# First 512 tokens by wide transposes: K-pair matmul groups over four banks and a chain of weight loads on the ACT queue, in a TensorE-bound kernel

## Chip, cores, metric

One core of one Trainium2 chip. The metric is the device time of one execution in microseconds, as a median over runs. The profile's own span of the same execution is about 1.7 to 2.2 us shorter (487.74 against 486.0 us for the kernel before), so spans are compared only with spans and device times only with device times.

## The reference, cut to what matters

```python
x = A_x                                        # 2048 tokens x 1024, bf16
g = sigmoid((x * gate_w).sum(-1))
a = linear_attention(x, A_wqkv) @ A_wo         # 32 heads of 32
b = dilated_local_attention(x, B_wqkv) @ B_wo  # window 8, dilation 2
out = g * a + (1 - g) * b
```

The kernel begins with the v projection of block B: `x @ B_wqkv[:, 2048:3072]`. It contracts over 1024 channels, in eight steps of 128 (called d here), so x has to stand transposed in SBUF, channels on the partitions. One matmul takes 128 tokens of one d as its stationary operand and 512 output columns as its moving one. 16 token tiles x 2 column halves x 8 steps make 256 matmuls for this projection.

## The kernel before

All operations are declared with a cost, an estimated transfer time and a priority. A list scheduler in Python, run when the kernel is built, orders each engine's queue by these numbers. So a change of costs or of priorities can reorder any engine. Transfers (DMA) are issued by the engines SP and ACT, each in its own queue. TensorE (PE) writes its sums to PSUM, which is used here in banks of 128 x 512 sums.

```python
def load_x(t, prio):          # one tile of 128 tokens, all eight d
    return P.op("sp", lambda e: e.dma_start_transpose(xT[:, :, t*128:(t+1)*128], x2[...]), 1.5, ..., lat=1.3)

load_x(0, 0)
load_w(0, 0, Bw, 2048, 0.1, 0, 2, "act")       # first weight half in pairs of d:
load_w(0, 0, Bw, 2048, 0.2, 2, 4, "act")       # two on the ACT queue,
load_w(0, 0, Bw, 2048, 0.3, 4, 6)              # two on the SP queue
load_w(0, 0, Bw, 2048, 0.4, 6, 8)
for t in range(1, NT):
    load_x(t, 3 + t)
for d in range(0, 8, 2):
    load_w(0, 1, Bw, 2560, 6.1 + 0.1*d, d, d + 2)   # second weight half, SP queue, behind x tile 3
...
for i in range(WARM):                          # WARM = 11 dummy matmuls
    P.op("pe", lambda e: e.matmul(banks[7].ap(), warm[:, 0:128], warm[:, :], start=True, stop=True), ...)
...
for t, half in [(4*b + i, half) for b in range(NT//4) for half in range(2) for i in range(4)]:
    bank = main.next()
    step = 2 if t == 0 else 8
    for d in range(0, 8, step):
        o = group(bank, xs, w, [...], d, d + step)
    ...
# much later: 16 small copies into zsel, and four "folds" woven into the next projection
            if n in (2, 4, 6, 8):
                fold((n - 2) // 4, (n - 2) // 2 % 2)
```

Four tiles go through the first column half, then the same four through the second, and so on. A tile of x is 256 KB, and so is a pair of d of a weight half. A pair of d is called a K-pair below, when the matmuls on it are meant. The late part belongs to block A: "kv" matmuls (az with pk), then the four folds of 16 small matmuls each (w with kvT), then "den" matmuls that read the tile zsel.

Of the kernel before, what the change touches and what calls it, by code (L numbers as in the profile page):

```python
# [13 lines left out]
D = 1024  # L14
# [1102 lines left out]
def build_kernel(nc, A_x, A_wqkv, A_wo, B_x, B_wqkv, B_wo, gate_w, out):  # L1117
    del B_x
    S = A_x.shape[1]
    NT = S // 128  # L1120
    HS = S // 2
    x2 = A_x[0].rearrange("(m e) d -> e m d", e=2)
# [5 lines left out]
    def SB(shape, dtype, name, at=None):  # L1128
        n = SZ[dtype]
        for d in shape[1:]:  # L1130
            n *= d
        if at is None:
            at = base[0]
            base[0] += (n + 31) // 32 * 32
        uid[0] += 1
        h = nc.alloc_sbuf_tensor_at("%s_%d" % (name, uid[0]), list(shape), dtype, offset=at)
        return Tile("S", h, at, list(shape), dtype)
# [38 lines left out]
    xT = SB([128, 8, S], BF16, "xT")  # L1176
    qT = SB([128, 8, S], BF16, "qT")
    kT = SB([128, 8, S], BF16, "kT")
    ws = [SB([128, 8, 1024], BF16, "w%d" % i) for i in range(4)]
# [12 lines left out]
    zsel = SB([128, 8, 32], BF16, "zsel")  # L1192
    kva = SB([128, 8, 33], F32, "kva")
# [25 lines left out]
    gwb = SB([128, 1024], BF16, "gwb", at=pk.t[3].lo)  # L1219
    xn = Ring([SB([128, 1024], BF16, "xn%d" % i, at=az.t[i].lo) for i in range(2)])  # L1220
# [7 lines left out]

    FILL = 0.2
    PVLAG = 3  # L1230
    WARM = 11
    PASSES = 6
    mm = lambda n: max(n / 2400.0, 0.0267) + 0.0025
    act = lambda n: 0.19 + n / 1200.0
    dps = lambda n: 0.14 + n / 960.0

    def plan(seen):

        P = Prog(nc, nc.alloc_semaphore)
# [63 lines left out]
        Bw = B_wqkv.rearrange("(dc p) f -> p dc f", p=128)  # L1303
        Bo = B_wo.rearrange("(dc p) f -> p dc f", p=128)

        def load_x(t, prio):
            e_, r = t // 8, t % 8
            return P.op("sp", lambda e: e.dma_start_transpose(xT[:, :, t * 128:(t + 1) * 128], x2[e_, r * 128:(r + 1) * 128, :]),  # L1308
                        1.5, writes=[xT.part((0, 8), (t * 128, (t + 1) * 128))], prio=prio, chan="x%d" % t, lat=1.3)

        def load_w(slot, half, src, c0, prio, d0=0, d1=8, eng="sp", after=()):
            n = d1 - d0
            return P.op(eng, lambda e: e.dma_start(ws[slot][:, d0:d1, half * 512:half * 512 + 512], src[:, d0:d1, c0:c0 + 512]), 0.4 + 0.2 * n,  # L1313
                        writes=[ws[slot].part((d0, d1), (half * 512, half * 512 + 512))], prio=prio, chan="w%d_%d_%d" % (slot, half, d0), lat=0.55 * n, after=after)

        load_x(0, 0)
        load_w(0, 0, Bw, 2048, 0.1, 0, 2, "act")
        load_w(0, 0, Bw, 2048, 0.2, 2, 4, "act")
        load_w(0, 0, Bw, 2048, 0.3, 4, 6)
        load_w(0, 0, Bw, 2048, 0.4, 6, 8)  # L1320
        for t in range(1, NT):
            load_x(t, 3 + t)
        for d in range(0, 8, 2):
            load_w(0, 1, Bw, 2560, 6.1 + 0.1 * d, d, d + 2)
        P.op("sp", lambda e: e.dma_start(gwb[:, :], gate_w[None, :].to_broadcast([128, D])), 0.6, writes=[gwb.all()], prio=29, chan="gw", lat=0.8)


        main = Pool(banks[0:7])

        def group(bank, lhs, rhs, reads, lo=0, hi=8):  # L1330
            def fn(e):
                last = None
                for dc in range(lo, hi):
                    last = e.matmul(bank.ap(), lhs(dc), rhs(dc), start=(dc == 0), stop=(dc == 7))  # L1334
                return last
            return P.op("pe", fn, (hi - lo) * mm(512), reads=reads, writes=[bank.iv])
# [13 lines left out]
        def x_tile(t):  # L1350
            return (lambda dc: xT[:, dc, t * 128:(t + 1) * 128]), xT.part((0, 8), (t * 128, (t + 1) * 128))
# [4 lines left out]
        def w_half(slot, half):  # L1356
            return (lambda dc: ws[slot][:, dc, half * 512:half * 512 + 512]), ws[slot].part((0, 8), (half * 512, half * 512 + 512))
# [13 lines left out]

        for i in range(WARM):
            P.op("pe", lambda e: e.matmul(banks[7].ap(), warm[:, 0:128], warm[:, :], start=True, stop=True), 0.43, reads=[warm.all()], writes=[banks[7].iv], prio=-1)


        early = {(2, 0): (1, 0, Bw, 1024, 21), (4, 1): (2, 0, Bw, 0, 22), (7, 1): (1, 1, Bw, 1536, 23), (10, 1): (2, 1, Bw, 512, 24),
                 (12, 1): (3, 0, Aw, 1024, 25), (14, 1): (3, 1, Aw, 1536, 26)}
        for t, half in [(4 * b + i, half) for b in range(NT // 4) for half in range(2) for i in range(4)]:
            vt, vs = vst.next()
            xs, xr = x_tile(t)  # L1380
            bank = main.next()
            w, wr = w_half(0, half)
            step = 2 if t == 0 else 8
            for d in range(0, 8, step):
                o = group(bank, xs, w, [xr, ws[0].part((d, d + step), (half * 512, half * 512 + 512))], d, d + step)
            move(vt[:, :, 0:32], lambda bank=bank: bank.ap().rearrange("p (h d) -> p h d", d=32), 512, bank, vt.part((0, 16), (0, 32)))
            P.op("sp", lambda e, t=t, vt=vt, half=half: e.dma_start(vB_hbm[t * 128:(t + 1) * 128, half * 528:half * 528 + 528], vt[:, :, :].rearrange("p h d -> p (h d)")), 0.6, reads=[vt.all()],
                 writes=[hb(t * 128, (t + 1) * 128, half)], chan="vst%d" % vs, lat=0.5, prio=5)
            if (t, half) in early:
                load_w(*early[t, half], after=[o])  # L1390
        load_w(0, 0, Aw, 2048, 30)
        load_w(0, 1, Aw, 2560, 31)


        for t in range(NT):
            xt, xs_ = xn.next()
            P.op("sp", lambda e, t=t, xt=xt: e.dma_start(xt[:, :], x2[t // 8, (t % 8) * 128:(t % 8) * 128 + 128, :]), 0.6, writes=[xt.all()], chan="xn%d" % xs_, lat=1.0)
            P.op("dve", lambda e, t=t, xt=xt: e.scalar_tensor_tensor(out=xt[:, :], in0=xt[:, :], scalar=1.0, in1=gwb[:, :], op0=ALU.mult, op1=ALU.mult,
                                                                      accum_out=gt[:, t:t + 1]), dps(1024), reads=[xt.all(), gwb.all()], writes=[xt.all(), gt.part((t, t + 1))],
                 prio=1000 + len(P.ops) + 80)  # L1400
# [7 lines left out]
        main = Pool(banks[0:4])  # L1408
# [109 lines left out]
        for e_ in range(2):  # L1518
            if True:
                for j in range(8):  # L1520
                    for isq in range(2):
                        for u in (2 * e_, 2 * e_ + 1):
                            bank = main.next()
                            w, wr = w_cols(1 + isq, j)
                            xs, xr = x_chunk(u)
# [10 lines left out]
        for c in range(4):  # L1536
            for I in range(2):
                P.op("sp", lambda e, c=c, I=I: e.dma_start(ws[1][32 * c:32 * c + 32, 4 * I:4 * I + 4, :],
                                                           A_wo[512 * I + 128 * c:512 * I + 128 * c + 128, :].rearrange("(r e) f -> e r f", e=32)), 0.6,
                     writes=[ws[1].part((4 * I, 4 * I + 4), (0, 1024))], prio=40, chan="wo%d_%d" % (c, I), lat=0.9)  # L1540
# [27 lines left out]
        for t in range(NT):  # L1568
            pkt, _ = pk.next()
            azt, _ = az.next()  # L1570
            xs, xr = x_tile(t)
            for r in range(4):
                bank = main.next()
                w, wr = w_half((3, 0)[r // 2], r % 2)
# [16 lines left out]
        main = Pool(banks)  # L1591
# [5 lines left out]
        for c in range(4):  # L1597
            for r in range(4):
                k = 4 * (c % 2) + r
                P.op("dve", lambda e, c=c, r=r, k=k: e.tensor_copy(zsel[32 * r:32 * r + 32, c:8:4, k:k + 1], kva[32 * c:32 * c + 32, r:8:4, 32:33]), 0.1,  # L1600
                     reads=[kva.all()], writes=[zsel.all()])

        def fold(I, jh):
            four = [main.next() for _ in range(4)]

            def fn(e):
                for r in range(4):
                    for c in range(4):
                        sl = 4 * I + r
                        last = e.matmul(four[c].ap()[32 * r:32 * r + 32, :], kvT[32 * c:32 * c + 32, 32 * sl:32 * sl + 32],  # L1610
                                        ws[1][32 * c:32 * c + 32, sl, jh * 512:(jh + 1) * 512], start=True, stop=True, tile_position=(32 * c, 32 * r))
                return last
            P.op("pe", fn, 0.3, mode="t", reads=[kvT.all(), ws[1].part((4 * I, 4 * I + 4), (jh * 512, jh * 512 + 512))], writes=[b.iv for b in four], name="fold")
            for c in range(4):
                move(ws[1][:, 4 * I + c, jh * 512:(jh + 1) * 512], four[c].ap, 512, four[c], ws[1].part((4 * I + c, 4 * I + c + 1), (jh * 512, jh * 512 + 512)))
# [92 lines left out]
        for n, (u, j) in enumerate(nums):  # L1708
            numer(u, j)
            if j == 7 and u % 2:  # L1710
                after(3, lambda u=u: over(u - 1, u))
            slot(0)
            if n in (2, 4, 6, 8):
                fold((n - 2) // 4, (n - 2) // 2 % 2)
            if n >= 20:
                a_out(*outs.pop(0))
                slot(0)
# [44 lines left out]
    P, flag_op = best[:2]  # L1762
# [55 lines left out]
```

## Time and profile before

| | before |
|---|---|
| device time, median | 487.27 us (487.18 to 487.52, 6 runs) |
| span of the profiled run | 486.0 us |
| TensorE (PE) busy | 474.7 us, 98% |
| first useful matmul | 6.25 us |
| last matmul ends | 483.0 us |

Two lines of the profile page: the busy time of each engine with its share of the span, and the shares by engine of the chain of work that ended last.

```profile
PE 474.7 (98%) x4339; PEld 223.0 (46%) x4403; DVE 285.2 (59%) x547; ACT 140.2 (29%) x227; POOL 5.9 (1%) x36
...
PE 95%; DVE 2%; issue 1%; DMA 1%; SPq 0%; ACT 0%
```

TensorE is busy nearly all the time and holds 95% of the chain. The change can only win back its idle time, or time in which it works without use.

The timeline of TensorE in the first 22 us (start, length, line, operation, shapes, number merged; in brackets the idle time before it and what ended it):

```profile
1.25 4.61 PE L1373 MATMUL ps_all<-warm 128*128 128x512 bf16 x11 [1.25 <-DVE warm L1283]
6.25 2.02 PE L1334 MATMUL ps_all<-w,xT 128*128 128x512 bf16 x8 [0.39 <-DMA xT<-in_A_x_dram]
8.51 6.65 PE L1334 MATMUL ps_all<-w,xT 128*128 128x512 bf16 x30 [0.24 <-DMA xT<-in_A_x_dram]
15.38 6.85 PE L1334 MATMUL ps_all<-w,xT 128*128 128x512 bf16 x31 [0.23 <-DMA w<-in_B_wqkv_dram]
```

The first line is the dummies: 11 matmuls start 0.43 us apart. Useful matmuls start 0.216 us apart once the clock is at full rate. These two spacings are how the clock shows in the timeline: 0.43 us is half rate. The next lines begin after short waits: for the first x, for the next x, for the weights' second half. (The trace lacks one matmul record in fifty: it has 251 of this projection's 256.)

The same view around the folds:

```profile
317.73 0.43 PE L1610 MATMUL ps_all<-w,kvT 32*32 32x512 bf16 x16
318.09 3.63 PE L1334 MATMUL ps_all<-xT,w 128*128 128x512 bf16 x16
322.22 0.44 PE L1610 MATMUL ps_all<-w,kvT 32*32 32x512 bf16 x16 [0.50 <-DVE pq L1347]
```

PE sat idle for 0.50 us before the second fold, and what ended it was a VectorE operation on the tile pq.

### The profile page before, as it was taken

To read this page: it belongs to the slowest core of one execution; us is meant where nothing else is said; L and a number is where in the kernel's file an instruction comes from. 1 tells how busy PE (TensorE), PEld (TensorE's weight loads), DVE (VectorE), ACT (ScalarE), POOL (GpSimd) and SP (SyncE) were. 2 spreads that over 40 slices of the span, in tenths; PEclk is the share of its full clock that TensorE was granted. 3 is DMA by queue.
4 is the path that set the end of the run, shared out by engine and by line. 5 is a ranking of instruction groups with operands and counts; after the bars stand their busy time and mean duration, and the time that the engine had idled before them with its cause. 6 is when DMAs were issued, how large, how long until landed. Compare 5 with 4: busy or idle time off the path is not lost.

```text
span 486.0 us, 10106 instructions
## 1 busy us (share of the span) xinstructions
PE 474.7 (98%) x4339; PEld 223.0 (46%) x4403; DVE 285.2 (59%) x547; ACT 140.2 (29%) x227; POOL 5.9 (1%) x36
## 2 busy tenths in 40 slices
PE   8999999999999999999999999999999999999997
PEld 3444444444444444454544454434444444444443
DVE  2121435888688888575666566496578236653434
ACT  2111121235322234334433333454532230111000
POOL 4000000000000000000000000000000000000000
PEclk9999999999999999999999999999999999999999
DMA  8999992232014459333222322810085018840212
GB/s 217 225 198 308 352 365 59 66 109 86 1 44 138 107 133 255 86 81 87 57 69 69 82 66 69 213 41 2 10 228 152 1 15 237 224 23 3 88 67 89
DMA packets 72951, 57.39 MB, mean 118 GB/s; under 512 B 37953, under 2 KB 60865, under 8 KB 72898
## 3 DMA queue, kind: packets, MB, share of 16 engines
q1 hardware_dynamic: 72210, 56.07, 43.7%
q8 instruction: 36, 0.59, 0.5%
q10 hardware_dynamic: 688, 0.59, 0.4%
q14 instruction: 17, 0.14, 0.1%
HBM read 34.49 MB, written 13.76 MB: 99 GB/s over the span
## 4 chain that ended last, share of the span: by engine, by line
PE 95%; DVE 2%; issue 1%; DMA 1%; SPq 0%; ACT 0%
PE ps_all L1334 78%; PE ps_all L1693 11%; PE ps_all L1463 2%; PE ps_all L1440 2%; DMA xT<-in_A_x_dram 1%; PE ps_all L1556 1%; DVE zsel L1600 1%; PE ps_all L1638 0%; DVE pq L1347 0%; SPq L1308 0%; DVE w L1365 0%; PE ps_all L1610 0%; SPq L1313 0%; ACT e L1341 0%; DVE e L1345 0%
## 5 line engine op out<-in xcount | busy, mean ns | idle before, releaser
L1334 PE MATMUL ps_all<-w,xT 128*128 128x512 bf16 x925 | 208.6, 379 | 4.1 <-issue 2.1
L1334 PE MATMUL ps_all<-xT,w 128*128 128x512 bf16 x746 | 166.3, 379 | 2.1 <-issue 1.4
L1334 PEld LDWEIGHTS ps_all<-w,xT 128*128 128x128 bf16 x960 | 91.4, 98 | 110.6 <-DMA xT<-in_A_x_dram 1.8
L1334 PEld LDWEIGHTS ps_all<-xT,w 128*128 128x128 bf16 x768 | 73.7, 98 | 88.9 <-issue 1.3
L1693 PE MATMUL ps_all<-w,qT 128*128 128x512 bf16 (+1 forms) x259 | 55.3, 372 | 0.3
L1693 PEld LDWEIGHTS ps_all<-w,qT 128*128 128x128 bf16 x264 | 25.9, 98 | 29.6
L1365 DVE CAST vst<-ps_all 128x512 bf16<-128x512 f32 x15 | 10.4, 694 | 43.6 <-PE ps_all L1334 43.6
L1345 DVE TENSOR_SCALAR e<-e 128x512 bf16<-128x512 bf16 x64 | 18.4, 290 | 27.7 <-ACT e L1343 15.1
L1448 ACT ACTIVATE E<-ps_all 128x1824 bf16<-128x1824 f32 (+1 forms) x18 | 30.4, 1688 | 13.4 <-PE ps_all L1440 11.7
L1697 DVE SCALAR_TENSOR_TENSOR o<-ps_all,gm,xT 128x512 bf16<-128x512 f32 (+1 forms) x25 | 18.0, 728 | 21.2 <-PE ps_all L1693 21.1
L1341 ACT ACTIVATE e<-ps_all 128x512 bf16<-128x512 f32 x32 | 19.1, 597 | 39.0 <-PE ps_all L1334 38.3
L1343 ACT ACTIVATE e<-ps_all 128x512 bf16<-128x512 f32 x32 | 19.1, 597 | 32.4 <-PE ps_all L1334 32.4
L1295 DVE TENSOR_TENSOR mx<-mx,kT 128x1024 bf16<-128x1024 bf16 x32 | 20.9, 688 | 10.4 <-ACT kT L1366 10.4
L1295 DVE TENSOR_TENSOR mx<-mx,qT 128x1024 bf16<-128x1024 bf16 x32 | 20.8, 688 | 8.0 <-ACT qT L1369 8.0
L1451 DVE TENSOR_TENSOR E<-E,msk 128x1824 bf16<-128x1824 bf16 (+1 forms) x18 | 19.9, 1104 | 7.8 <-ACT E L1448 7.4
L1366 ACT ACTIVATE vst<-ps_all 128x512 bf16<-128x512 f32 x17 | 10.2, 600 | 48.0 <-PE ps_all L1334 48.0
L1480 DVE TENSOR_TENSOR ot<-ps_all,rs 128x512 bf16<-128x512 f32 x36 | 23.3, 686 | 0.0
L1366 ACT ACTIVATE az<-ps_all 128x512 bf16<-128x512 f32 x22 | 13.2, 600 | 34.5 <-PE ps_all L1334 34.5
L1366 ACT ACTIVATE kT<-ps_all 128x512 bf16<-128x512 f32 x20 | 11.9, 596 | 38.2 <-PE ps_all L1334 38.2
L1347 DVE SCALAR_TENSOR_TENSOR pk<-ps_all,e 128x512 bf16<-128x512 f32 x32 | 21.9, 689 | 0.7
L1369 ACT ACTIVATE qT<-ps_all 128x512 bf16<-128x512 f32 x19 | 11.3, 597 | 37.4 <-PE ps_all L1334 37.3
L1369 ACT ACTIVATE xT<-ps_all,g 128x512 bf16<-128x512 f32 x10 | 6.9, 687 | 45.1 <-PE ps_all L1334 45.1
(72 smaller groups left out, 261.1 us busy)
## 6 DMA issues: line engine op xcount, KB each, us to landing
rb<-rc_hbm SPq DMA_DIRECT2D x32, 256.0 KB, 5.0
w<-in_A_wqkv_dram SPq DMA_DIRECT2D x6, 1024.0 KB, 8.6
v<-vB_hbm SPq DMA_DIRECT2D x36, 132.0 KB, 2.8
vB_hbm<-vst SPq DMA_DIRECT2D x32, 132.0 KB, 6.0
w<-in_B_wqkv_dram SPq DMA_DIRECT2D x4, 1024.0 KB, 8.8
xn<-in_A_x_dram SPq DMA_DIRECT2D x16, 256.0 KB, 2.8
out_dram<-o SPq DMA_DIRECT2D x15, 256.0 KB
oB_hbm<-ot SPq DMA_DIRECT2D x36, 96.0 KB, 2.3
```

Source lines behind the costliest of these rows:

```text
L1295: P.op("dve", lambda e, m=m, op=op: e.tensor_tensor(m[:, 0:n], m[:, 0:n], src, op), 0.08 + n / 1920.0, reads=[m.all(), reg], writes=[m.all()],
L1334: last = e.matmul(bank.ap(), lhs(dc), rhs(dc), start=(dc == 0), stop=(dc == 7))
L1341: P.op("act", lambda e: e.activation(e_[:, :], bank.ap(), ACT.Exp), act(512), reads=[bank.iv], writes=[e_.all()])
L1343: P.op("act", lambda e: e.activation(e_[:, :], bank.ap(), ACT.Exp, accum_out=qe[:, col:col + 1]), act(512) + 0.1, reads=[bank.iv], writes= ...
L1345: P.op("dve", lambda e: e.tensor_scalar(e_[:, :], e_[:, :], 1.0, 1e-6, op0=ALU.min, op1=ALU.add), 0.25, reads=[e_.all()], writes=[e_.all()])
L1347: P.op("dve", lambda e: e.scalar_tensor_tensor(out=dst, in0=bank.ap(), scalar=0.0, in1=e_[:, :], op0=ALU.max, op1=ALU.add), dps(512), read ...
L1366: fa = lambda e: e.activation(dst, src(), ACT.Copy)
L1369: fa = lambda e: e.activation(dst, src(), ACT.Copy, scale=scale)
L1448: P.op("act", lambda e: e.activation(E[:, 0:32 * nq].rearrange("p (j q) -> p j q", j=4), ps[:, 4:8, 0:8 * nq], ACT.Exp), act(32 * nq), rea ...
L1451: P.op("dve", lambda e: e.tensor_tensor(ev(), ev(), m[:, :, :].rearrange("p r q -> p (r q)")[:, None, :].to_broadcast([128, 16, 2 * nq]), ...
L1480: P.op("dve", lambda e, r=r, bv=bv, h=h: e.tensor_tensor(o[:, 512 * h:512 * h + 512].rearrange("p (k i c) -> p k i c", k=2, c=32), bv()[:, ...
L1693: last = e.matmul(bank.ap(0, f1 - f0), qT[:, dc, t * 128:(t + 1) * 128], ws[3][:, dc, f0:f1], start=(dc == 0), stop=(dc == 7))
```

## The change

The intent: start useful work as soon as an eighth of the data is there. The first 512 tokens come by four wide transposes, each of 512 tokens x two steps of d. PE takes them pair of d by pair of d, for four token tiles in four PSUM banks. The weight pairs are issued on the ACT queue, the third when the first has landed, the fourth when the second has landed, and the second half right behind the fourth. Eight tiles, not four, go through the first half before the second is needed. There are 8 dummies in place of 11. At the other end, the zsel copies get a lower priority and the folds come one step later.

```diff
-    WARM = 11
+    WARM = 8
...
-        load_x(0, 0)
-        load_w(0, 0, Bw, 2048, 0.1, 0, 2, "act")
...
+        o_w = []
         for d in range(0, 8, 2):
-            load_w(0, 1, Bw, 2560, 6.1 + 0.1 * d, d, d + 2)
+            o_w.append(load_w(0, 0, Bw, 2048, 0.1 + 0.1 * d, d, d + 2, "act", o_w[-2:-1]))
+            P.op("sp", lambda e, d=d: e.dma_start_transpose(xT[:, d:d + 2, 0:512], x2[0, 0:512, 128 * d:128 * d + 256]),
+                 1.3, writes=[xT.part((d, d + 2), (0, 512))], prio=d / 2, chan="xd%d" % d, lat=1.2)
+        for t in range(4, 8):
+            load_x(t, 4 + t)
...
-        for t, half in [(4 * b + i, half) for b in range(NT // 4) for half in range(2) for i in range(4)]:
+        for t, half in [(t, half) for t0, n in ((0, 8), (8, 4), (12, 4)) for half in range(2) for t in range(t0, t0 + n)]:
...
+            if t < 4 and half == 0:
+                if t == 0:
+                    first = [main.next() for _ in range(4)]
+                    for d in range(0, 8, 2):
+                        for t_ in range(4):
+                            o = group(first[t_], x_tile(t_)[0], w, [...], d, d + 2)
+                    for d in range(0, 8, 4):
+                        load_w(0, 1, Bw, 2560, 3 + 0.1 * d, d, d + 4, "act", o_w[-1:])
+                bank = first[t]
+            else: ...
+                if (t, half) == (5, 0):          # x tiles 8 to 15, gate loads: only after this group
+                    x_op = o
+                    for t_ in range(8, NT):
+                        load_x(t_, 4 + t_, [o])
...
-                P.op("dve", ... zsel copy ..., 0.1, ...)
+                P.op("dve", ... zsel copy ..., 0.16, ..., prio=1000 + len(P.ops) + 100)
...
-            if n in (2, 4, 6, 8):
-                fold((n - 2) // 4, (n - 2) // 2 % 2)
+            if n in (3, 5, 7, 9):
+                fold((n - 3) // 4, (n - 3) // 2 % 2)
```

(Also changed: the estimated transfer times that the list scheduler uses, and the place of one later weight load.)

More of the change, by code (lines that the diff above doesn't have):

```diff
@@ L1304, in plan, with load_x @@
         Bo = B_wo.rearrange("(dc p) f -> p dc f", p=128)
-        def load_x(t, prio):
+        def load_x(t, prio, after=()):
             e_, r = t // 8, t % 8
             return P.op("sp", lambda e: e.dma_start_transpose(xT[:, :, t * 128:(t + 1) * 128], x2[e_, r * 128:(r + 1) * 128, :]),
-                        1.5, writes=[xT.part((0, 8), (t * 128, (t + 1) * 128))], prio=prio, chan="x%d" % t, lat=1.3)
+                        1.5, writes=[xT.part((0, 8), (t * 128, (t + 1) * 128))], prio=prio, chan="x%d" % t, lat=1.15, after=after)
         def load_w(slot, half, src, c0, prio, d0=0, d1=8, eng="sp", after=()):
@@ L1313, in load_w @@
             return P.op(eng, lambda e: e.dma_start(ws[slot][:, d0:d1, half * 512:half * 512 + 512], src[:, d0:d1, c0:c0 + 512]), 0.4 + 0.2 * n,
-                        writes=[ws[slot].part((d0, d1), (half * 512, half * 512 + 512))], prio=prio, chan="w%d_%d_%d" % (slot, half, d0), lat=0.55 * n, after=after)
-        load_x(0, 0)
-        load_w(0, 0, Bw, 2048, 0.1, 0, 2, "act")
-        load_w(0, 0, Bw, 2048, 0.2, 2, 4, "act")
-        load_w(0, 0, Bw, 2048, 0.3, 4, 6)
-        load_w(0, 0, Bw, 2048, 0.4, 6, 8)
-        for t in range(1, NT):
-            load_x(t, 3 + t)
-        for d in range(0, 8, 2):
-            load_w(0, 1, Bw, 2560, 6.1 + 0.1 * d, d, d + 2)
-        P.op("sp", lambda e: e.dma_start(gwb[:, :], gate_w[None, :].to_broadcast([128, D])), 0.6, writes=[gwb.all()], prio=29, chan="gw", lat=0.8)
+                        writes=[ws[slot].part((d0, d1), (half * 512, half * 512 + 512))], prio=prio, chan="w%d_%d_%d" % (slot, half, d0), lat=0.42 * n, after=after)
+        o_w = []
+        for d in range(0, 8, 2):
+            o_w.append(load_w(0, 0, Bw, 2048, 0.1 + 0.1 * d, d, d + 2, "act", o_w[-2:-1]))
[3 more added lines that the diff above has]
+            load_x(t, 4 + t)
         main = Pool(banks[0:7])
@@ L1373, in plan @@
             P.op("pe", lambda e: e.matmul(banks[7].ap(), warm[:, 0:128], warm[:, :], start=True, stop=True), 0.43, reads=[warm.all()], writes=[banks[7].iv], prio=-1)
-        early = {(2, 0): (1, 0, Bw, 1024, 21), (4, 1): (2, 0, Bw, 0, 22), (7, 1): (1, 1, Bw, 1536, 23), (10, 1): (2, 1, Bw, 512, 24),
+        early = {(1, 1): (1, 0, Bw, 1024, 21), (4, 1): (2, 0, Bw, 0, 22), (7, 1): (1, 1, Bw, 1536, 23), (10, 1): (2, 1, Bw, 512, 24),
                  (12, 1): (3, 0, Aw, 1024, 25), (14, 1): (3, 1, Aw, 1536, 26)}
-        for t, half in [(4 * b + i, half) for b in range(NT // 4) for half in range(2) for i in range(4)]:
+        for t, half in [(t, half) for t0, n in ((0, 8), (8, 4), (12, 4)) for half in range(2) for t in range(t0, t0 + n)]:
             vt, vs = vst.next()
             xs, xr = x_tile(t)
-            bank = main.next()
             w, wr = w_half(0, half)
-            step = 2 if t == 0 else 8
-            for d in range(0, 8, step):
-                o = group(bank, xs, w, [xr, ws[0].part((d, d + step), (half * 512, half * 512 + 512))], d, d + step)
+            if t < 4 and half == 0:
[3 more added lines that the diff above has]
+                        for t_ in range(4):
+                            o = group(first[t_], x_tile(t_)[0], w, [xT.part((d, d + 2), (t_ * 128, t_ * 128 + 128)), ws[0].part((d, d + 2), (0, 512))], d, d + 2)
+                    for d in range(0, 8, 4):
+                        load_w(0, 1, Bw, 2560, 3 + 0.1 * d, d, d + 4, "act", o_w[-1:])
+                bank = first[t]
+            else:
+                bank = main.next()
+                o = group(bank, xs, w, [xr, ws[0].part((0, 8), (half * 512, half * 512 + 512))])
+                if (t, half) == (5, 0):
+                    x_op = o
+                    for t_ in range(8, NT):
+                        load_x(t_, 4 + t_, [o])
             move(vt[:, :, 0:32], lambda bank=bank: bank.ap().rearrange("p (h d) -> p h d", d=32), 512, bank, vt.part((0, 16), (0, 32)))
@@ L1390, in plan @@
                 load_w(*early[t, half], after=[o])
+        P.op("sp", lambda e: e.dma_start(gwb[:, :], gate_w[None, :].to_broadcast([128, D])), 0.6, writes=[gwb.all()], prio=29, chan="gw", lat=0.8, after=[x_op])
         load_w(0, 0, Aw, 2048, 30)
@@ L1396, in plan @@
             xt, xs_ = xn.next()
-            P.op("sp", lambda e, t=t, xt=xt: e.dma_start(xt[:, :], x2[t // 8, (t % 8) * 128:(t % 8) * 128 + 128, :]), 0.6, writes=[xt.all()], chan="xn%d" % xs_, lat=1.0)
+            P.op("sp", lambda e, t=t, xt=xt: e.dma_start(xt[:, :], x2[t // 8, (t % 8) * 128:(t % 8) * 128 + 128, :]), 0.6, writes=[xt.all()], chan="xn%d" % xs_, lat=1.0, after=[x_op])
             P.op("dve", lambda e, t=t, xt=xt: e.scalar_tensor_tensor(out=xt[:, :], in0=xt[:, :], scalar=1.0, in1=gwb[:, :], op0=ALU.mult, op1=ALU.mult,
@@ L1599, in plan @@
                 k = 4 * (c % 2) + r
-                P.op("dve", lambda e, c=c, r=r, k=k: e.tensor_copy(zsel[32 * r:32 * r + 32, c:8:4, k:k + 1], kva[32 * c:32 * c + 32, r:8:4, 32:33]), 0.1,
-                     reads=[kva.all()], writes=[zsel.all()])
+                P.op("dve", lambda e, c=c, r=r, k=k: e.tensor_copy(zsel[32 * r:32 * r + 32, c:8:4, k:k + 1], kva[32 * c:32 * c + 32, r:8:4, 32:33]), 0.16,
+                     reads=[kva.all()], writes=[zsel.all()], prio=1000 + len(P.ops) + 100)
         def fold(I, jh):
```

## The prediction

> **What bounds the kernel now.** TensorE. The engine table has it busy 474.7 of 486.0 us (98%), the chain of waits is 95% PE. In the timeline, 512-column matmuls start 0.216 us apart from 15.38 us to the end at 483.0 us. A change of the first loads can only win back idle PE time, about 11 us: the head; some forty gaps of 0.16 us around the attention blocks; one of 0.50 us at 322 us; 3 us of tail. The change touches the head and the piece at 322 us.
>
> **The head before, from the timeline and the DMA issues.** Eleven dummy matmuls run from 1.25 to 5.86 us, 0.43 us apart, at half rate; the rate doubles at about 5.5 us. The first transpose of x (issued at 0.80 us) lands at 6.20 us, the weight pairs at 3.65, 6.01, 6.77 and 7.62 us, the next transposes at 8.47, 9.49 and 10.51 us. Useful work starts at 6.25 us. The 38 matmuls to 15.38 us take 9.13 us; at 0.216 us they need 8.2. So three waits (a weight pair at 7.6, x at 8.5, the weights' second half at 15.1 us) cost 0.9 us.
>
> **What the change does.**
> - A wide transpose is 256 KB in the same 256-byte packets (1,024 for an old one), so I expect the old issue cost, 1.25 to 1.4 us, and about 1 us of transfer.
> - After the first pair of x and weights there are 32 matmuls over four banks, 8 per pair: 1.73 us of PE for 512 KB. Transposes can be issued every 1.3 us and DMA moved 250 to 300 GB/s there, so pairs land every 1.3 to 1.8 us, about as fast as PE eats them. The third and fourth weight pair wait for the first and second (3.65 and 6.0 us), early enough.
> - The second weight half is first needed 64 matmuls (13.8 us) after the start, not 32: the wait at 15.1 us goes.
> - The first weight pairs and transpose are issued at the same times as before; only the third weight pair no longer contends. I expect the first landing at 5.3 to 6.2 us, estimate 5.8: a gain of 0.4 us.
> - Eight dummies end at about 4.7 us. The Trainium skill ("TensorE: Matmul & The Clock Gate", Part 1) says that activity in a free-running window of about 3.4 us releases the clock. The trace agrees roughly (4.2 us of dummies before the rate doubled). With a hole before the data a few matmuls may run at half rate: 0.2 us each, estimate 0.2 in total, at worst 1 to 2 us.
> - The sixteen copies to zsel (0.17 us each on DVE, in the chain from 315 to 318.6 us) get a lower priority and the folds start one step later; that should remove the 0.50 us for which PE waited on pq at 322 us.
> - Later loads have several us of slack.
>
> **Sum.** 0.9 + 0.4 + 0.5 - 0.2 = 1.6 us, all on the PE chain. Predicted 485.7 us, range 484.2 to 487.3. Chances: faster by over 2% 0.01, within 2% 0.98, slower by over 2% 0.01.
>
> **What would show it.** First useful matmul between 5.3 and 6.2 us; the 64th ends 13.8 to 14.2 us later with no gap above 0.2 us; no wait on weights near 15 us; no idle PE before the folds near 320 us; everything after shifted earlier by the sum.
>
> **What would make it wrong.** Wide transposes that take longer to issue or land (rows of 512 bytes instead of 2 KB), which start PE later and starve it at each pair; a clock at half rate for a whole further window; the weight chain landing pairs three and four late; a new order from the list scheduler that opens or closes gaps in the middle.

## The result

| | before | changed |
|---|---|---|
| device time, median | 487.27 us (487.18 to 487.52) | 489.03 us (487.55 to 489.34) |
| ratio, changed over before | | 1.0029 (95%: 1.0016 to 1.0042) |
| span of the profiled run | 486.0 us | 487.2 us |
| first useful matmul | 6.25 us | 5.73 us |
| k projection begins | 62.22 us | 64.18 us |
| last matmul ends | 483.02 us | 484.40 us |

A ratio here is the mean time of one kernel's runs over the mean of the other's in the same rounds, so it is not quite the ratio of the medians. Executions over 1.5% slower than the fastest of the same kernel are left out of the means. The changed kernel is slower by some 0.3%, and its runs spread over 1.8 us where the old ones spread over 0.34 us. (On the chips of the later calls the kernel before spread over 0.75 to 2.0 us too, so the wider spread is not shown to be the change's.)

The page of the changed kernel:

```profile
PE 475.7 (98%) x4336; PEld 223.4 (46%) x4400; DVE 289.3 (59%) x554; ACT 135.6 (28%) x220; POOL 5.9 (1%) x36
...
PE 94%; SPq 2%; DMA 2%; issue 1%; ACT 0%; DVE 0%
```

PE is busy one microsecond longer with three matmuls fewer (the dummies), and SP's issuing and DMA now hold 2% each of the chain. The timeline of TensorE:

```profile
1.25 3.59 PE L1370 MATMUL ps_all<-warm 128*128 128x512 bf16 x8 [1.25 <-DVE warm L1283]
5.73 12.82 PE L1331 MATMUL ps_all<-w,xT 128*128 128x512 bf16 x47 [0.88 <-DMA xT<-in_A_x_dram]
19.27 2.98 PE L1331 MATMUL ps_all<-w,xT 128*128 128x512 bf16 x13 [0.72 <-DMA xT<-in_A_x_dram]
```

Useful work starts 0.52 us earlier. But its first line takes 12.82 us for 48 matmuls (one record missing), which at 0.216 us are 10.4 us; and there is a wait for x in front of the matmul at 19.27 us. Stretches of 2 us of the changed kernel show the first part (start:end, length, then busy time and number of instructions of PE, PEld, DVE, ACT, POOL, then granted clock, DMA share and GB/s):

```profile
6.00:8.00 2.00, 2.00 (x6) 0.73 (x5) 0.43 (x2) 0.00 (x0) 0.42 (x2) 1.00 1.24 285
8.00:10.00 2.00, 2.00 (x7) 0.64 (x5) 0.00 (x0) 0.00 (x0) 0.00 (x0) 1.00 1.23 101
```

PE is busy for the whole of both stretches, but starts 6 and 7 matmuls in them where a stretch at full rate has 11. The single records are 0.43 us apart from 5.73 to 10.38 us: half rate. Note that the column of the granted clock says 1.00 there. The first clock record of this trace, a release to full rate, is at 10.41 us, and the column does not know what came before it. Early in a kernel, read the spacing and not that column.

The second part is in the chain that ended last (start, length, what):

```profile
0.80 1.37 SPq L1319
...
2.23 1.34 SPq L1319
...
3.61 1.58 SPq L1319
...
5.22 1.86 SPq L1319
...
7.13 1.31 SPq L1308
...
8.48 3.22 SPq L1308
...
11.74 7.49 DMA xT<-in_A_x_dram
...
19.27 9.46 PE ps_all L1331 x43
```

The chain in the head runs through SP only: six transposes are issued one behind the other, 1.3 to 3.2 us each, until the seventh, x tile 6, is issued at 11.74 us. It takes 7.49 us to land, and PE goes on at 19.27 us. Beside it, on the ACT queue, the second weight half is issued in two pieces:

```profile
11.91 0.97 ACTq L1313 DMA_DIRECT2D w<-in_B_wqkv_dram  x2
```

The half-rate matmuls are not in this chain at all: even at full rate PE would have had to wait for this tile. An estimate from this trace: at full rate and with the same landings, PE would have waited 1.25 us for the fourth K-pair (due at 10.91 us, landed at 12.12) and 1.93 us for x tile 6 (due at 17.34 us, PE going on at 19.27). That is 3.18 us, as much as the 2.29 us of half rate and the 0.88 us of wait that were paid. So in this trace the clock cost nothing on top of the late data.

The folds, as the profile has them after:

```profile
321.41 0.43 PE L1620 MATMUL ps_all<-w,kvT 32*32 32x512 bf16 x16
321.78 3.63 PE L1331 MATMUL ps_all<-xT,w 128*128 128x512 bf16 x15
325.34 0.43 PE L1620 MATMUL ps_all<-w,kvT 32*32 32x512 bf16 x16
```

The wait of 0.50 us is gone. From the last kv matmul (314.05 and 316.01 us) to the first den matmul (346.08 and 347.47 us) the changed kernel takes 0.57 us less: 31.46 against 32.03 us. So this part of the change works, and the head loses more than it gains here.

A bookkeeping of the head that the six traces below obey: take the start of the k projection, subtract the start of the first useful matmul, the excess of half-rate matmuls over 0.216 us each, and the waits. What is left is the 256 matmuls of the v projection.

| trace | first useful | excess at half rate | waits | k projection begins | left |
|---|---|---|---|---|---|
| before | 6.25 | 0 | 0.71 | 62.22 | 55.26 |
| changed | 5.73 | 2.29 | 0.88 | 64.18 | 55.28 |
| changed, second trace (below) | 5.78 | 0 | 2.97 | 63.99 | 55.24 |
| second half on SP, 11 dummies | 5.69 | 0 | 1.74 | 62.69 | 55.26 |
| K-pairs in order, 11 dummies | 5.92 | 0.54 | 0 | 61.72 | 55.26 |
| K-pairs in order, 8 dummies | 5.92 | 2.22 | 0 | 63.41 | 55.27 |

So the head of the changed kernel lost 1.96 us in this trace: 0.52 and 0.71 won, 2.29 and 0.88 paid. The folds gave 0.57 back, and about 0.2 more was won behind the last matmul. The 2.29 is what half rate took, not what it added to the time: see the estimate above.

### The profile page after: what moved, and what is told of

Its sections match the earlier page's. It is cut to its first block, busy times and chain, and to the rows that moved or that the text cites. A ratio compares the mean times of both kernels' runs of the same rounds, so it can differ in the third digit from the quotient of the medians.

```text
span 487.2 us, 10096 instructions
## 1 busy us (share of the span) xinstructions
PE 475.7 (98%) x4336; PEld 223.4 (46%) x4400; DVE 289.3 (59%) x554; ACT 135.6 (28%) x220; POOL 5.9 (1%) x36
## 4 chain that ended last, share of the span: by engine, by line
PE 94%; SPq 2%; DMA 2%; issue 1%; ACT 0%; DVE 0%
PE ps_all L1331 77%; PE ps_all L1703 11%; PE ps_all L1473 2%; PE ps_all L1450 2%; DMA xT<-in_A_x_dram 2%; SPq L1319 1%; PE ps_all L1566 1%; SPq L1308 1%; PE ps_all L1648 0%; PE ps_all L1620 0%; ACT e L1338 0%; DVE o L1707 0%
## 5 line engine op out<-in xcount | busy, mean ns | idle before, releaser
L1366 ACT ACTIVATE qT<-ps_all 128x512 bf16<-128x512 f32 x17 | 10.2, 598 | 40.1 <-PE ps_all L1331 40.1
L1440 DVE TENSOR_SCALAR qd<-qT,par 128x912 bf16<-128x912 bf16 (+1 forms) x34 | 14.6, 452 | 10.5 <-PE ps_all L1450 9.5
L1363 ACT ACTIVATE kT<-ps_all 128x512 bf16<-128x512 f32 x17 | 10.2, 598 | 38.0 <-PE ps_all L1331 38.0
```

Of the source, the lines that this page charges most:

```text
L1363: fa = lambda e: e.activation(dst, src(), ACT.Copy)
```

## The experiments

Two theories. **Clock theory**: with 8 dummies the array idles for about 0.9 us before the data come, so the clock is released one window later. **DMA theory**: data come too late for the new order of matmuls, and the clock costs nothing since PE would wait anyway. Of the DMA theory there are two forms: the order of the transfers is wrong, or the throughput is too small whatever the order.

| run | edit | median us | before, same chip | ratio (95%) |
|---|---|---|---|---|
| e1 | changed, 11 dummies | 488.63 | 487.50 | 1.0023 (1.0005 to 1.0040) |
| e2 | before, 8 dummies | 487.76 | 487.50 | 1.0006 (0.9992 to 1.0021) |
| e3 | before + folds and zsel part | 486.89 | 487.50 | 0.9984 (0.9972 to 0.9996) |
| e4 | e1, narrow transposes (reordered, see below) | 489.12 | 487.50 | 1.0045 (1.0025 to 1.0065) |
| e0 | changed, again | 488.14 | 487.18 | 1.0015 (1.0002 to 1.0028) |
| e5 | e1, second half on SP behind x7 | 486.91 | 487.18 | 0.9994 (0.9981 to 1.0007) |
| e6 | e5 with 8 dummies | 487.80 | 487.18 | 1.0016 (1.0003 to 1.0029) |
| e7 | e5, narrow transposes (reordered) | 489.31 | 487.18 | 1.0064 (1.0035 to 1.0092) |
| e8 | both halves in K-pairs (reordered) | 490.13 | 487.43 | 1.0048 (1.0029 to 1.0068) |
| e9 | e8 with 8 dummies | 489.16 | 487.43 | 1.0040 (1.0021 to 1.0058) |
| e10 | e8 without the weight chain | 490.31 | 487.43 | 1.0053 (1.0028 to 1.0078) |
| e11 | e8 with PE's order fixed | 486.76 | 487.50 | 0.9986 (0.9973 to 0.9999) |
| e12 | e11 with 8 dummies | 487.65 | 487.50 | 1.0000 (0.9985 to 1.0014) |
| e13 | e3 again | 486.96 | 487.50 | 0.9990 (0.9978 to 1.0003) |
| e14 | e7 with PE's order fixed | 489.71 | 487.50 | 1.0049 (1.0018 to 1.0080) |

All gave correct results.

### e1: the dummies alone

```diff
-    WARM = 8
+    WARM = 11
```

> Only the dummy matmuls go back from 8 to 11; the order tool shows every engine otherwise unchanged. Clock theory (the hole of 0.9 us before the data leaves the array at half rate for a further window, which cost 2.3 us in the traced run): no useful matmul at half rate spacing, or two at most, first useful one at about 5.9 us, and a median 1 to 2 us below the changed kernel's 489.0, so 487.0 to 488.0, with the run to run spread back from 1.8 us to about 0.4 us. Rival, the DMA theory (x tile 6 landed at 19.2 us and PE would have waited for it anyway): the half-rate matmuls vanish but the wait in front of x tile 6 grows from 0.9 to about 2 us or more and a new one of about 1 us opens before the fourth K-pair, so the median stays within 0.5 us of 489.0.

Measured: 488.63 us (486.99 to 489.64), ratio 1.0023; the changed kernel itself had 1.0029 on its chip. In the profiled run no useful matmul ran at half rate, but PE waited 1.14 us for x tile 5 (landed at 15.43 us) and 0.30 us for x tile 6. The spread did not shrink. So bringing the dummies back alone gains nothing that can be told from noise, as the DMA theory expected. Two of its expectations missed in this trace: the wait for x tile 6 did not grow to 2 us (tile 5 was hit in its place), and no wait before the fourth K-pair showed. The trace is also of one of the two fast runs of six (487.14 us); the other four took 488.4 to 489.6 us.

### e2: the dummies alone, on the kernel before

```diff
-    WARM = 11
+    WARM = 8
```

> The kernel before with 8 dummies in place of 11, nothing else changed. Clock theory: the first x lands at 6.2 us, the dummies end at about 4.7 us, so a hole of 1.5 us; useful matmuls start at half rate for up to a window of 3.4 us or more: slower than before by 1 to 2.5 us (488.3 to 489.8), with more spread between runs. Rival (eight dummies are enough to release the clock; the slow start in the changed kernel is due to its wide matmul order or its operands): same time as before within 0.3 us.

Measured: 487.76 against 487.50 us, ratio 1.0006. The expected loss of 1 us or more did not come. In the profiled run the clock was released at 4.61 us, before the data, so that trace says nothing of a late release. The kernel before waits for transfers between 6 and 9 us anyway; that this hides a late release is argued, not shown.

### e3 and e13: the folds alone

```diff
-                ... zsel copy ..., 0.1,
-                     reads=[kva.all()], writes=[zsel.all()])
+                ... zsel copy ..., 0.16,
+                     reads=[kva.all()], writes=[zsel.all()], prio=1000 + len(P.ops) + 100)
-            if n in (2, 4, 6, 8):
-                fold((n - 2) // 4, (n - 2) // 2 % 2)
+            if n in (3, 5, 7, 9):
+                fold((n - 3) // 4, (n - 3) // 2 % 2)
```

> The kernel before plus only the zsel priority and the folds one step later. Theory: the 0.50 us wait before the second fold at 322 us goes, the rest is the same: 0.4 to 0.6 us faster than before, about 486.7. Rival: the gain of 0.58 us seen in the changed kernel's trace after 311 us is an accident of its other order: no gain.

> The kernel before plus only the zsel priority and the later folds, again, on this chip: 0.4 to 0.8 us faster than before.

Measured: ratio 0.9984 and, on another chip, 0.9990, which is 0.8 and 0.5 us; the second interval just reaches 1. In the traces the stretch from the last kv matmul to the first den matmul is 31.46 us (e3, e13) where the kernel before has 32.03. It is 31.45 or 31.46 in all 15 traces of kernels with this part, and 32.03 and 32.05 in the two without (before, e2). The gain belongs to this part and not to an accident of the order.

### e4: narrow transposes in the changed kernel

```diff
-            P.op("sp", ... wide transpose of d, d + 1, 512 tokens ...)
+            load_x(d // 2, d / 2)
-                    for d in range(0, 8, 2):
-                        for t_ in range(4):
+                    for t_ in range(4):
+                        for d in range(0, 8, 2):
```

> The changed kernel with 11 dummies, but the first 512 tokens again by four narrow transposes of 128 tokens, tile by tile in four K-pair steps; the weight chain on the ACT queue and the second weight half behind it are kept. If the wide transposes with K-pair groups are what the DMA chokes on (about 70 to 170 GB/s in the trace between 8 and 10 us), this one is faster than the same kernel with wide transposes by 0.5 us or more and its fourth transpose lands before 11 us. If the second weight half competing with x tiles 6 and 7 is what delays them, both have the same wait before x tile 6 (landing near 19 us) and times within 0.4 us of each other.

Measured: 489.12 us. This run cannot answer what it was built for: the list scheduler put half of each of tiles 0 to 3 before the rest of tile 0, so PE needed x tile 3 after 12 matmuls and waited 1.25 us for it. What it does show: x tile 5 again landed late (16.93 us, issued at 8.8) next to the second weight half (16.69 and 18.32 us), so the wide form is not what made those tiles late here.

### e0: the changed kernel, a second trace

> The changed kernel as it is, as a control on the chip of this call. Both theories: 0 to 2 us slower than before, a spread of 1.5 us or more; a wait in front of x tile 5 or 6 of 0.5 us or more in the trace; half-rate useful matmuls only if the clock record shows a release later than the first useful matmul.

```profile
5.78 5.34 PE L1331 MATMUL ps_all<-w,xT 128*128 128x512 bf16 x24 [0.93 <-DMA xT<-in_A_x_dram]
11.93 5.34 PE L1331 MATMUL ps_all<-w,xT 128*128 128x512 bf16 x23 [0.82 <-DMA xT<-in_A_x_dram]
18.59 1.90 PE L1331 MATMUL ps_all<-w,xT 128*128 128x512 bf16 x8 [1.32 <-DMA xT<-in_A_x_dram]
20.83 1.46 PE L1331 MATMUL ps_all<-w,xT 128*128 128x512 bf16 x6 [0.34 <-DMA xT<-in_A_x_dram]
```

This run shows that waits for data alone are enough for the loss. The clock record shows the release at 4.71 us, before the first useful matmul, and no useful matmul is at half rate. Yet the span is 487.2 us, as in the first trace. In place of half-rate matmuls there are waits: 0.98 us for the fourth K-pair, 1.48 us for x tile 6, 0.51 us for x tile 7. That fits the estimate for the first trace: there the half-rate matmuls filled time that would have been waits.

### e5: the second weight half behind x tiles 4 to 7

```diff
-                        load_w(0, 1, Bw, 2560, 3 + 0.1 * d, d, d + 4, "act", o_w[-1:])
+                        load_w(0, 1, Bw, 2560, 11.5 + 0.1 * d, d, d + 4)
```

> The changed kernel with 11 dummies and the second weight half (1 MB) issued on the SP queue behind x tiles 4 to 7, in place of the ACT queue as soon as the first half has landed. Order theory (that megabyte, not needed before 64 matmuls, overtakes x tiles 5 to 7, which are needed after 40 to 56): x tiles 5 to 7 land before 15 us, no wait longer than 0.3 us in front of them, and 1 to 2 us faster than the changed kernel, at or below the time of before. Rival (the DMA engines simply have too little throughput in this stretch, whatever the order): the wait moves to the second weight half near 19 us and the time stays within 0.5 us of the changed kernel.

```profile
5.69 5.35 PE L1331 MATMUL ps_all<-w,xT 128*128 128x512 bf16 x24
11.88 8.79 PE L1331 MATMUL ps_all<-w,xT 128*128 128x512 bf16 x39 [0.84 <-DMA xT<-in_A_x_dram]
21.25 1.02 PE L1331 MATMUL ps_all<-w,xT 128*128 128x512 bf16 x4 [0.57 <-issue]
```

The transpose of x tile 6 in the view of the tile xT:

```profile
L1308 SPq DMA_TRANSPOSE xT<-in_A_x_dram x1: 1311/1311/1311, 11.3 to 11.3; - x1
DMA to landing us min/median/max: 3.9/3.9/3.9
```

Measured: 486.91 us where the changed kernel had 488.14 on the same chip, 1.2 us faster. But these two differ by two edits, the place of the load and the three dummies. The place alone is e5 against e1 (ratios 0.9994 and 1.0023, on two chips) with 11 dummies, and e6 against e0 (below) with 8. x tile 6 landed at 15.23 us, 3.9 us after it was issued, where it took 7.5 us in the changed kernel. The other traces say the same: with the second half on the ACT queue tile 6 took 7.5, 7.2, 6.9 and 8.8 us (changed, e0, e1, e4), with it on the SP queue behind tile 7 it took 3.9, 4.3 and 3.9 us (e5, e6, e7). The waits in front of x tiles 5 to 7 are gone (tiles 6 and 7 landed at 15.23 and 16.20 us, later than the 15 us expected, but before their turn). That is what the order theory expected of the landings. But its rival is half right: a wait of 0.73 us appears at 21.25 us, for the second weight half, which now lands at 21.16 us, and the wait of 1.0 us before the fourth K-pair stays.

### e6: the same with 8 dummies

```diff
-    WARM = 11
+    WARM = 8
```

> The same as the one with the second weight half on the SP queue, but with the 8 dummies of the change; every engine's order is otherwise the same. Clock theory: with the wait on x gone the half-rate matmuls are no longer hidden: 0.5 to 2 us slower in the median than with 11 dummies and a wider spread, as the release falls in some runs one window later. Rival (the eight dummies cost nothing because DMA sets the pace of the first 15 us anyway): within 0.3 us of each other.

Measured: 487.80 against 486.91 us, 0.9 us slower, though in the profiled run the clock was released early (4.15 us) and that run was the fastest of the five. The two ratios' intervals overlap slightly (1.0003 to 1.0029, 0.9981 to 1.0007). So with the wait on x out of the way the missing dummies seem to cost, though this trace does not show how. Note also e6 against the changed kernel on the same chip (e0), which differ by the place of the load alone: 487.80 against 488.14 us, ratios 1.0016 and 1.0015. With 8 dummies, moving the load gains nothing clear either; in e6's trace PE waited 1.18 us for the second half, which landed at 20.51 us.

### e7: narrow transposes with the loads of e5

> Narrow transposes tile by tile, 11 dummies, and the second weight half on the SP queue behind x tiles 4 to 7. It tells what the wide transposes with K-pair groups are worth once the order of the loads is right. If they help: this one has waits before x tiles 1 to 3 of 1 to 2 us in all and is 0.5 to 1.5 us slower than its wide twin with 11 dummies. If they are of no use: the same within 0.3 us.

Measured: 489.31 us, with runs up to 493. As in e4, the list scheduler had reordered PE (waits of 0.64 and 1.55 us for x tiles 2 and 3). It tested the wrong thing and was built again as e14.

### e8, e9, e10: a version meant to beat both, first try

The second half is taken in K-pairs too, in the old order of tiles (four of half 0, four of half 1), and is loaded in pairs on the SP queue right behind the wide transposes:

```diff
-        for t, half in [(t, half) for t0, n in ((0, 8), (8, 4), (12, 4)) for half in range(2) for t in range(t0, t0 + n)]:
+        for t, half in [(t, half) for t0 in range(0, NT, 4) for half in range(2) for t in range(t0, t0 + 4)]:
-            if t < 4 and half == 0:
+            if t < 4:
...
-                    for d in range(0, 8, 4):
-                        load_w(0, 1, Bw, 2560, 3 + 0.1 * d, d, d + 4, "act", o_w[-1:])
+                    for d in range(0, 8, 2) if half == 0 else ():
+                        load_w(0, 1, Bw, 2560, 3.5 + 0.1 * d, d, d + 2)
```

e9 has 8 dummies; e10 drops the chain (`o_w[-2:-1]`) from the weight pairs of the first half.

> A version meant to beat both: wide transposes and K-pair groups as in the change, 11 dummies, the tile order of before (four tiles of half 0, the same four of half 1), with the second weight half also taken in K-pairs over four banks and loaded in four pairs on the SP queue right behind the wide transposes, ahead of x tiles 4 to 7. Order theory (what matters is that each transfer lands in the order of demand; here about 256 KB are needed per 8 matmuls, 1.73 us, from the first pair of the second half on): only the wait before the fourth K-pair remains (0 to 1.0 us, as measured), no wait after 13 us; the switch to the k projection begins near 61.3 us against 62.2 before; 485.7 to 486.5, so 0.7 to 1.5 us faster than before. Rival (throughput of the DMA engines is the limit whatever the order): waits of 1 us or more appear before the pairs of the second half between 12 and 18 us, and the time is no better than 487.

> The same with 8 dummies, all else the same instruction by instruction. Clock theory: where the release falls before 5.6 us nothing is lost, where it falls a window later 1.5 to 2.3 us; median 0.5 to 1.5 us slower than with 11 dummies, spread over 1 us. Rival (DMA sets the pace): within 0.3 us.

> The same with 11 dummies, but the four weight pairs of the first half are issued on the ACT queue at once, without the chain of landings. If the chain is what makes the fourth K-pair late (its weight pair was issued at 5.5 us and landed at 9.4 to 11.9 us): the wait before the fourth pair goes, 0.3 to 1.0 us faster where it occurred, though the first x lands up to 0.6 us later. If the wait comes from the transfers of the wide transposes themselves: the fourth transpose lands at 10.5 us or later as before and the time is the same or a little worse.

All three were slower, 489.16 to 490.31 us. The PE order shows why: from its estimates the list scheduler had put matmuls of the second half before the third K-pair, so that after 16 matmuls PE waited for the second half. In the timeline of e8:

```profile
5.88 3.61 PE L1331 MATMUL ps_all<-w,xT 128*128 128x512 bf16 x16 [0.27 <-DMA xT<-in_A_x_dram]
11.68 10.49 PE L1331 MATMUL ps_all<-w,xT 128*128 128x512 bf16 x40 [2.18 <-DMA w<-in_B_wqkv_dram]
```

After a wait of 2.34 us (2.18 us of idle time in this view) the spacing went to 0.43 us again: the clock record says half rate from 11.77 to 15.18 us. The comparison of 11 and 8 dummies is worthless here (in e9's trace the wait was 2.01 us and the clock stayed up). e10 does tell one thing by its landings. Without the chain, the second wide transpose landed at 10.50 us, and in e8, with it, at 6.49 us. Issued all at once, the weight pairs got ahead of the transposes in this trace, which speaks for the chain; in the median the two do not differ (490.31 and 490.13 us).

### e11: the same with PE's order fixed

```diff
-        def group(bank, lhs, rhs, reads, lo=0, hi=8):
+        def group(bank, lhs, rhs, reads, lo=0, hi=8, after=()):
...
-                            o = group(first[t_], ..., d, d + 2)
+                            o = group(first[t_], ..., d, d + 2, [o] if t_ + d + half else ())
```

> The version meant to beat both, now with the TensorE order of the first 64 matmuls fixed by dependences (pairs 0 to 3 of half 0, then pairs 0 to 3 of half 1). Order theory: second-half pairs land near 11.6, 12.4, 13.1 and 13.8 us as in the misordered version, all before their turn (12.6, 14.3, 16.1, 17.8 us); x tiles 4 to 7 land before 19 us, before their turn; only the wait before the fourth pair is left (0 to 1.2 us); the switch to the k projection near 61 to 61.8 us; 485.6 to 486.6, 0.7 to 1.6 us faster than before and 0.1 to 1 us faster than the fold part alone. Rival (throughput is the limit whatever the order): waits of 1 us or more after 12 us, no better than the fold part alone.

```profile
1.25 4.88 PE L1370 MATMUL ps_all<-warm 128*128 128x512 bf16 x11 [1.25 <-DVE warm L1283]
5.92 16.25 PE L1331 MATMUL ps_all<-w,xT 128*128 128x512 bf16 x72
```

From 5.92 us on there is not one wait. The pairs of the second half landed at 11.52 to 13.67 us, x tiles 4 to 7 at 14.70 to 18.87 us, all before their turn. The k projection begins at 61.72 us, 0.50 us before the kernel before, and the span is 484.6 us. (The trace of the kernel before had a late first x, at 6.20 us; in e13, which has the old head and got it at 5.48 us, the k projection begins at 61.91 us.) The median of 486.76 us, ratio 0.9986, is a little above the range expected for it (485.6 to 486.6): still the fastest median, but against the folds alone on the same chip (e13, 486.96 us) only 0.2 us, less than the runs' spread. So in this order every transfer of the head came in time, and throughput was not the limit. What is won in the head is small, since the old head lost only 0.71 us to waits.

Even with 11 dummies this trace paid 0.54 us for the clock: its release was at 7.01 us.

### e12: the same with 8 dummies

> The same with 8 dummies, all else the same. Clock theory: median 0.3 to 1.5 us slower than with 11 dummies, spread of 1 us or more between runs. Rival (no cost): within 0.3 us.

The timelines of e12 and stretches of 2 us of e12 and of e11:

```profile
1.25 3.59 PE L1370 MATMUL ps_all<-warm 128*128 128x512 bf16 x8 [1.25 <-DVE warm L1283]
5.92 16.43 PE L1331 MATMUL ps_all<-w,xT 128*128 128x512 bf16 x65 [1.07 <-DMA xT<-in_A_x_dram]
```

```profile
6.00:8.00 2.00, 2.00 (x5) 0.63 (x6) 0.43 (x2) 0.00 (x0) 0.40 (x2) 1.00 1.21 311
8.00:10.00 2.00, 2.00 (x6) 0.73 (x5) 0.00 (x0) 0.00 (x0) 0.00 (x0) 1.00 1.16 252
```

```profile
6.00:8.00 2.00, 2.00 (x9) 0.79 (x8) 0.43 (x2) 0.00 (x0) 0.40 (x2) 1.00 1.14 286
8.00:10.00 2.00, 2.00 (x11) 0.94 (x10) 0.00 (x0) 0.00 (x0) 0.00 (x0) 1.00 1.19 244
```

In e12 there are 5 and 6 matmuls in these two stretches, in e11 9 and 11. The release came at 10.46 us in e12 and at 7.01 us in e11: 3.45 us apart, about one window (a drop in mid-kernel lasted 3.41 us in e8), as if both had the same window grid and the hole of about 1 us (the last dummy ends at 4.84 us, the data's first matmul starts at 5.92 us) had spoilt the window before 7.05 us. It cost 2.22 us in this trace, and 0.9 us in the median (487.65 against 486.76 us), the same as between e6 and e5. Two pairs of kernels, equal but for three dummies, agree; but the intervals of each pair overlap, so a cost of the missing dummies is likely and not proven.

### e14: narrow transposes with PE's order fixed

```diff
-                            o = group(first[t_], ..., d, d + 2)
+                            o = group(first[t_], ..., d, d + 2, [o] if t_ + d else ())
```

> Narrow transposes, 11 dummies, second weight half on the SP queue behind x tiles 4 to 7, eight tiles of half 0 first, with the TensorE order fixed to tile by tile. Against the same with wide transposes (486.9 on its chip, ratio to before 0.9994): if the wide form with K-pair groups is worth its place, this one starts tile 0 no later but waits 0.5 to 1 us more for the third and fourth weight pair and x tiles 1 to 3, so ratio 1.000 to 1.002. If the narrow form is as good: ratio 0.998 to 1.000.

```profile
7.53 0.60 PE L1330 MATMUL ps_all<-w,xT 128*128 128x512 bf16 x2 [0.50 <-DMA w<-in_B_wqkv_dram]
11.05 11.14 PE L1330 MATMUL ps_all<-w,xT 128*128 128x512 bf16 x43 [2.92 <-DMA w<-in_B_wqkv_dram]
```

```profile
10.00:12.00 2.00, 0.95 (x4) 0.41 (x5) 0.00 (x0) 0.31 (x1) 0.00 (x0) 0.95 1.28 243
12.00:14.00 2.00, 2.00 (x6) 0.76 (x5) 0.00 (x0) 0.29 (x1) 0.00 (x0) 0.50 0.92 134
```

Measured: 489.71 us, in two clusters (488.2 to 488.3 and 491.2 to 493.1 us): slower than either expectation. The narrow form with the chain needs the fourth weight pair after 6 matmuls and gets it at 11.00 us: a wait of 3.08 us. The clock column then reads 0.50: after this wait the array was back at half rate, from 11.79 to 15.20 us by the clock record. So the chain of weight pairs does not fit this tile-by-tile order. Wide transposes, K-pairs and the chain belong together; taken as a set with a good order of the rest (e11), they are worth about as much as the old head.

## Why the prediction was wrong, point by point

- **First useful matmul at 5.3 to 6.2 us**: right (5.73 us). But the gain of 0.4 us put down to it is not the change's. The head of the kernel before, in the traces of e2, e3 and e13, got its first x at 5.48 to 5.74 us too; 6.20 us was one draw.
- **Old waits of 0.9 us go**: they measured 0.71 us (a missing matmul record had been read as a wait), and they did go.
- **Folds, 0.5 us**: right; 0.57 us in the trace, 0.5 to 0.8 us in e3 and e13.
- **Clock, "0.2 in total, at worst 1 to 2 us"**: the mechanism was named, the size was off: 2.29 us in the first trace, where late data hid it, and about 0.9 us in the median where it is not hidden (e5 and e6, e11 and e12). Whether it is paid is luck: it was in two of the six traces with 8 dummies (changed and e12, holes of 0.88 and 1.07 us). In e0, e2 and e6 the holes were as long (0.93, 0.80 and 1.05 us), but the release had come just before them, at 4.71, 4.61 and 4.15 us.
- **"Later loads have several us of slack"**: this is the step that failed, and with it the price of "the wait at 15.1 us goes": that wait did go, but the load that was moved for it delayed others. At full rate from 5.73 us on x tile 6 was due at about 16.1 us, and it landed at 19.23 us. The prediction asked when the second weight half would be needed (64 matmuls after the start) and not when it would be issued: on the ACT queue, as soon as the first half had landed. In the first trace that was at 11.9 us, next to x tile 6 (11.74 us), which is needed after 48 matmuls; the weights' packets ran from 13.0 us on, those of tile 6 only from 14.3 us. In e1 it was at 9.5 us and hit tile 5. The Trainium skill ("DMA: Bandwidth & Descriptors", section "Issuing engines are not separate DMA queues") says that DMAs issued from different engines run on the same 16 DMA engines and interleave. The traces agree: x tile 6 took 7.5 us to land beside that megabyte, and 3.9 us without it (e5). From 14.5 to 16 us of the first trace the queue of the weights moved 0.26 MB and that of the transposes 0.07 MB. So an early load on an idle queue was not free here.
- **"About as fast as PE eats them"**: true of the first three pairs. The fourth landed between 10.1 and 12.1 us in the traces with the chain, and its turn is at about 10.9 us, so up to 1.0 us of wait. DMA moved 101 GB/s between 8 and 10 us in the changed kernel's trace and 222 in that of e1, with the same loads up to 9.4 us. Why these slow stretches come and go between runs was not found, so this second failed step has no shown cause.
- **The sum**: it was built as if the terms were independent. They are not. In the first trace the half-rate matmuls took the place of waits for data; the second trace of the same kernel had the waits and no half-rate matmuls and ended at the same span of 487.2 us. Bringing the dummies back alone (e1) gained nothing clear, and nor did moving the load alone (e6); both together (e5) gained 1.2 us on the same chip, with intervals that just overlap (0.9981 to 1.0007 and, for e0, 1.0002 to 1.0028). Nor was there much to win: the folds alone (e3, e13) are as fast as e5, and the best head (e11) beats them by 0.2 us.

## What to carry to other kernels

When a start-up phase is rearranged, list for every transfer the matmul that needs it and check that transfers are issued in the order of these needs, over all queues together; here a load issued early on another queue delayed those that were needed first. Two stalls that overlap can hide each other, so test fixes in combination, and do not take the one that a single trace shows for the cause. Where a scheduler orders the instructions from estimates, check the order that came out before a run: five experiments here (e4, e7, e8, e9 and e10) tested something else than they were built for.

## What the Trainium skill lacked or had wrong

- "TensorE: Matmul & The Clock Gate", Part 1, gives a free-running window of about 3.4 us, and the traces agree: each drop in mid-kernel lasted 3.41 us (11.77 to 15.18 us in e8). It does not say how much idle time a window may hold and still release the clock. Counting back in steps of 3.41 us from each release: the window that ended with the release held 0.61 us of idle time in e9; the window before that one held 0.88 us in the changed kernel (3.58 to 7.00 us) and 1.07 us in e12 (3.63 to 7.05 us), and the clock stayed at half rate after it. The release came anywhere from 4.15 to 7.01 us in the traces with at least 11 dummies or a lucky window, and at 10.41 and 10.46 us in two with 8.
- The same page, "Why this matters for your kernels", warns of idle gaps over about 3 us. Here a wait of 2.34 us was enough to lose the full clock (e8), and one of 2.01 us was not (e9). Whether the length of a wait decides or its part in one window, these runs do not separate.
- No page says that the profile's granted-clock column reads 1.00 before the first clock record: in the changed kernel's trace matmuls ran 0.43 us apart up to 10.38 us under a column of 1.00.
- "DMA: Bandwidth & Descriptors" gives no issue time for a transpose of this size on trn2 (its one figure per instruction is for small tiles). Here one of 256 KB, wide or narrow, held the SP queue for 1.28 us in the median (the twelve of one tile in the changed kernel; 1.37 and 1.34 us for its first two wide ones), which would cap back-to-back transposes at about 200 GB/s (an estimate: 262 KB over 1.3 us), and for longer when others were in flight: 3.22 us behind five in the changed kernel, 5.85 us behind seven in e4.
